# Two elementwise products of a rational activation moved from VectorE to GpSimd

## The chip, the cores and the metric

The kernel runs on one core of a Trainium2 chip. The metric is the device time of one execution in microseconds (us); the time before is the median of three executions.

## The reference

The program computes banded attention, a dense mixture of experts, and a feed-forward layer with a rational activation. The last one is where the change lies; `a` has four numbers, `b` two.

```python
def _moe2_ref(x, w_in, w_out, a, b):
    h = x @ w_in                      # 1152 x 512 by 512 x 2048
    h2 = h * h
    h3 = h2 * h
    P = a[0] + a[1] * h + a[2] * h2 + a[3] * h3
    Q = 1.0 + np.abs(b[0]) * np.abs(h) + np.abs(b[1]) * h2
    g = P / (Q + 1e-06)
    return (g @ w_out).astype(np.float32)
```

## The kernel before, in words

Tokens run in three chunks c = 0, 1, 2 of 384 columns. Hidden features run in units of 256, two units to a granule g; granules 0 to 7 (units 0 to 15) belong to the experts, granules 8 to 11 (units 16 to 23) to the rational layer. Float32 operands of the large products are split into a high and a low part, and three passes carry high by high, high by low and low by high. So an activation has two products: `hh`, the high part, and `hl`, the low part.

A unit of a chunk, written (u, c) here, goes like this. TensorE makes its hidden features in one PSUM tile (`h_bank`, L319, 48 matmuls for two units). The activation then makes `hh` and `hl`. Later TensorE multiplies these by the second weights, a token tile at a time (`o_half`, L356): for each of three token tiles, unit u's `hh` four times, its `hl` twice, then unit u+1's `hh` four times and its `hl` twice. DVE adds the result to the sum (`o_sum`, L384 or L386).

The activation is the class `Rational` (L418 to L467). Its steps, named after its methods, are:

- `first`: three ScalarE instructions (L430 to L432) that read the PSUM tile: the square, |b0 h|, and the start of the numerator.
- `denominator`: one DVE instruction (L435) that joins square and absolute value, then Ln and Exp on ScalarE (L439, L440).
- `numerator`: two DVE instructions (L444, L445), each with one operand in PSUM. The second frees the PSUM tile.
- `third`: two DVE instructions (L450, L453), a Newton step on the reciprocal, both operands in SBUF.
- `fourth`: one DVE instruction (L458), both operands in SBUF, and ScalarE's copy that makes `hh` (L462).
- `fifth`: one DVE instruction (L465) that makes `hl` from the result and `hh`.

Each engine takes its instructions in the order in which the program is written (`manual_schedule`, L469). `h_step` and `o_step` (L614, L638) set that order. An even unit's `denominator`, `numerator` follow at once behind its `first`, but behind `third` and `fourth` of the odd unit of the pair before; the odd unit's `fifth` comes between the even unit's `denominator` and `numerator`. The even unit's `third`, `fourth`, `fifth` and the odd unit's `denominator`, `numerator` are put between the token tiles of the next `o_step`. In the steady part a period is two units and three token tiles, 16.54 us. The entry into the rational layer (L661 to L675, and the `extra` turns of x at L690 to L692) and the last chunk (L715 to L755) are written out by hand.

Of the kernel before, what the change touches and what calls it, by code (L numbers as in the profile page):

```python
"""Banded attention, a dense mixture of experts and a rational-activation MLP, in one launch.

Tokens run in three chunks of 384 columns; the middle one has the first 192 tokens of both batches.
For a chunk, a plain head has six blocks of 64 queries against 96 keys, and a dilated head eight of
48 queries against 80 keys, two for each residue of the position, within which its band is plain.
Float32 operands of the large products are split into two float32r parts each
(x = hi + lo exactly), and three passes carry hi*hi + hi*lo + lo*hi.
"""
# [2 lines left out]

# [17 lines left out]
NT, DM = 1152, 512  # L29
E, FE = 4, 1024  # L30
F2 = 2048
# blocks of a chunk, their queries and their keys: plain and dilated heads
BLOCKS = ((6, 64, 96), (8, 48, 80))
TC = 384
NCH = 3
# [1 line left out]
WINDOW, DIL = 32, 4  # L37
NG1, NG = 2 * E, 2 * E + F2 // 512
QSCALE = 1.0 / D ** 0.5
NORMAL64 = float(np.uint32(897 << 20).view(np.float32))  # high word of the double 2**-126  # L40


@with_exitstack
def body(ctx, tc, qkv, mask, dp, w1, w2, w1d, w2d, coef, out):
# [10 lines left out]
    third = []  # L55

    def h_tile(count=[0]):
        """Two banks; a third pair joins once the attention has left it."""
        count[0] += 1
        pool = third[0] if third and count[0] % 3 == 0 else psh  # L60
        return pool.tile([128, 2, 512], F32, tag="h", name="ps_h")
# [11 lines left out]

    nc.scalar.preload_act_table_set("natural_log_exp_and_others")

# [1 line left out]
    w1s, w2s, scratch = {}, {}, {}  # L77

    def load_w(src, store, nm):
# [28 lines left out]
    split_w1, split_w2 = split_w(w1s, "w1"), split_w(w2s, "w2")  # L108

    def weight(store, u, n):  # L110
        """hi and lo of a unit's weights as n row groups."""
        return (store[u][:, i].rearrange("p (k f) -> p k f", k=n) for i in range(2))

# [1 line left out]
    def convert(pool):  # L115
        pieces = []
        for u in range(2 * NG1, 2 * NG, 2):
            for nm, src in (("w1", w1d), ("w2", w2d)):
                for v_ in (u, u + 1):
                    scratch[nm, v_] = dram.tile([128, 2, 1024], F32, tag=f"{nm}_{v_}", name=f"{nm}_{v_}")  # L120
                    for i in range(2):
                        pieces.append((src[v_ - 2 * NG1], scratch[nm, v_], slice(i * 512, (i + 1) * 512)))

        def load(n):
            src, _, s = pieces[n]
            x = pool.tile([128, 512, 2], U32, tag="x64", name="x64")
            nc.sync.dma_start(x.rearrange("p a b -> p (a b)"), src.bitcast(U32)[:, 2 * s.start:2 * s.stop])
            return x

        nxt = load(0)  # L130
        for n, (_, dst, s) in enumerate(pieces):
            x, nxt = nxt, load(n + 1) if n + 1 < len(pieces) else None
            low, high = x[:, :, 0], x[:, :, 1]
            t = pool.tile([128, 512], U32, tag="t", name="t")
            e = pool.tile([128, 512], U32, tag="e", name="e")
            f = pool.tile([128, 512], F32, tag="f", name="f")
            mag = pool.tile([128, 512], F32, tag="mag", name="mag")
            w = pool.tile([128, 2, 512], F32R, tag="w", name="w")
            nc.scalar.activation(mag, high.bitcast(F32), AF.Abs)
            # sign, exponent and the upper 20 bits of the fraction  # L140
            nc.vector.tensor_scalar(
                out=t, in0=high, scalar1=3, scalar2=0x3FFFFFF8,
                op0=ALU.logical_shift_left, op1=ALU.bitwise_and,
            )
            yield
            nc.vector.scalar_tensor_tensor(
                out=t, in0=high, scalar=0xC0000000, in1=t, op0=ALU.bitwise_and, op1=ALU.bitwise_or
            )
            yield
            # the lower 32 bits of the fraction, scaled by the signed power of two  # L150
            nc.vector.tensor_scalar(
                out=e, in0=t, scalar1=0xFF800000, scalar2=None, op0=ALU.bitwise_and
            )
            nc.vector.scalar_tensor_tensor(
                out=f, in0=low, scalar=2.0 ** -52, in1=e.bitcast(F32), op0=ALU.mult, op1=ALU.mult
            )
            yield
            nc.vector.tensor_tensor(out=f, in0=f, in1=t.bitcast(F32), op=ALU.add)
            yield
            # below float32's normal range: zero  # L160
            nc.vector.scalar_tensor_tensor(  # L161
                out=f, in0=mag, scalar=NORMAL64, in1=f, op0=ALU.is_ge, op1=ALU.mult
            )
            nc.scalar.copy(w[:, 0], f)  # L164
            yield
            nc.vector.tensor_tensor(out=w[:, 1], in0=f, in1=w[:, 0].bitcast(F32), op=ALU.subtract)  # L166
            nc.sync.dma_start(dst[:, :, s], w.bitcast(F32))
            yield

# [1 line left out]
    xt = {}  # L171

    def new_x(c):
# [2 lines left out]
        xt[c] = (xh, xl)  # L176

    class Attn:
        """A chunk's pair of heads; the steps up to the transposes run a head (half) at a time.

        A block's scores have its queries on partitions, those of odd blocks from 64 up.
        """

        def __init__(self, c, p):
            self.c, self.p = c, p
# [120 lines left out]
                    out=dst(xl), in0=src, in1=dst(xh.bitcast(F32)), op=ALU.subtract  # L306
                )

# [1 line left out]
    hs = {}  # L310
    acc = {}

# [32 lines left out]
        return [(0, 128, 128 * t)]  # L345

    def o_half(g, t, v, ps):
        """A token tile's products with one unit's 256 features."""
        c, j = divmod(t, 3)
        tk = slice(j * 128, (j + 1) * 128)  # L350
        hh, hl = hs[2 * g + v, c]
# [9 lines left out]
        return pso.tile([128, 512], F32, tag="o", name="ps_o")  # L361

    def o_tile(g, t, ps=None):
        """A token tile's products with a granule; the sum too, unless the caller's bank holds them."""
        held, ps = ps is not None, ps if ps is not None else o_bank()
        for v in range(2):
            o_half(g, t, v, ps)
        if not held:
            o_sum(g, t, ps)
# [21 lines left out]
    x2_ps = {}  # L391

    def x2_turn(c, half):
        """Two of the four feature groups of a chunk, turned features-first."""
        if half == 0:
            new_x(c)
        ps = x2_ps[c, half] = h_tile()
# [18 lines left out]
        x2_split(c, half)  # L416

    class Rational:  # L418
        """g = P(h) / (Q(h) + 1e-6): 1/Q from exp(-ln Q) and a Newton step, P negated with it."""
        pool = None  # L420

        def __init__(self, u, c, ps):
            self.u, self.c, self.ps = u, c, ps

        def first(self):
            ps = self.ps[:, :, :TC]
            self.sq = self.pool.tile([128, 2, TC], F32, tag="sq", name="sq")
            self.ab = self.pool.tile([128, 2, TC], F32, tag="ab", name="ab")
            self.u1 = self.pool.tile([128, 2, TC], F32, tag="u1", name="u1")
            nc.scalar.activation(self.sq, ps, AF.Square)  # L430
            nc.scalar.activation(self.ab, ps, AF.Abs, scale=absb[:, 0:1])  # L431
            nc.scalar.activation(self.u1, ps, AF.Identity, scale=na[:, 3:4], bias=na[:, 2:3])  # L432

        def denominator(self):
            nc.vector.scalar_tensor_tensor(  # L435
                out=self.sq, in0=self.sq, scalar=absb[:, 1:2], in1=self.ab,
                op0=ALU.mult, op1=ALU.add,
            )
            nc.scalar.activation(self.ab, self.sq, AF.Ln, bias=cbias)  # L439
            nc.scalar.activation(self.ab, self.ab, AF.Exp, scale=-1.0)  # L440

# [20 lines left out]
            nc.scalar.copy(self.hh, self.u1)  # L462

        def fifth(self):
            nc.vector.tensor_tensor(  # L465
                out=self.hl, in0=self.u1, in1=self.hh.bitcast(F32), op=ALU.subtract
            )  # L467

    with tc.manual_schedule():  # L469
# [9 lines left out]
        ps_h = {}  # L479

        def h_k(k, u):
            """The k-th quarter of granule 0 on chunk 0."""
            if k == 0:
                ps_h[u] = h_tile()
            for i in range(2):
# [57 lines left out]
            21: [part(split_w2, 3, 1)],  # L543
        }

        # TensorE's clock falls when little of it is used, as in the first steps of the attention
        warm = const.tile([128, 512], BF16, name="warm")
        nc.vector.memset(warm, 0.0)
        ps_w = h_tile()
# [98 lines left out]
        for g in range(NG):  # L648
# [63 lines left out]
                x2_half(0, 0)  # L712
                x2_half(0, 1)
            o_step(g, 1)
        # the last chunk's hidden features come before the products that wait for nothing  # L715
        u, g = 2 * NG - 2, NG - 1
        r = []
        for v in range(2):
            r.append(Rational(u + v, 2, h_tile()))
            for i in range(2):  # L720
                h_bank(u + v, 2, i, r[v].ps)
            for f in between.pop(0):
# [36 lines left out]


def _slots():
    """Where each chunk's pair of heads starts in the array of windows, and the array's size."""
    at, slot = 0, {}
    for c in range(NCH):
        for p in range(NPAIR):
# [7 lines left out]


def _window(c, kind, b):
    """Batch, queries and keys (S for none) of a block."""
    _, qb, kb = BLOCKS[kind]
    if kind == 0:
        t = 64 * (b % 3) if c == 1 else 192 + 64 * b
# [7 lines left out]


def _mask():
    """Added to the raw scores: nothing, or -1e9 before the scale."""  # L790
    from ml_dtypes import bfloat16

    m = np.zeros((2, 64, 4, 320), np.float32)
# [59 lines left out]
```

## Time and profile before

| | us |
|---|---|
| time, median of 3 executions (667.65 to 669.11) | 668.04 |
| profiled execution, span from first to last instruction | 667.8 |
| TensorE matmul busy in the span | 654.5 (98%) |
| DVE busy | 496.5 (74%) |
| ScalarE (ACT) busy | 269.1 (40%) |
| GpSimd (POOL) busy | 17.6 (3%) |
| granted TensorE clock, mean | 0.994 |

The profile gives the profiled execution's span alone; its time is this span and what lies around it, about 0.2 us by the median. Matmuls are pipelined, so TensorE's busy share is not its share of peak; what is read here is where it waits. PE is TensorE's matmul, PEld its weight load. A row of the timeline reads: start, duration, engine, line, operation, result and operands, and in brackets how long the engine was idle before and what ended that.

### The profile page before, as it was taken

Reading aid. Unit: us, or ns where it says so; the run is one execution under the profiler, and the core shown is the slowest. Engines: PE = TensorE matmul, PEld = TensorE weight load, DVE = VectorE, ACT = ScalarE, POOL = GpSimd, SP = SyncE. Lnnn points to the kernel's source line nnn. Section 1 sums busy time; section 2 is a strip of 40 time slices with the busy share of each in tenths; the row PEclk is TensorE's granted clock in tenths of the full one; section 3 lists DMA queues with packets and bytes.
Section 4 is the critical chain, followed back from the end, with each engine's and each line's share of the span. In section 5 each row is a group of like instructions: output and inputs, shape, how many; then the busy total and the mean of one; then the engine's idle time right before and its main releaser. Section 6 shows DMA issues by size and latency. Waiting matters only on the chain.

```text
span 667.8 us, 9561 instructions
## 1 busy us (share of the span) xinstructions
PE 654.5 (98%) x3845; PEld 586.5 (88%) x3845; DVE 496.5 (74%) x760; ACT 269.1 (40%) x510; POOL 17.6 (3%) x30
## 2 busy tenths in 40 slices
PE   6899999999999999999999999999999999999997
PEld 4788889899999999999999999999999999999985
DVE  3597653796886786786786786634899999999986
ACT  3465441242232332332322322214656555555551
POOL 1111110000000000000000000000000000000000
PEclk9799999999999999999999999999999999999999
DMA  8746201262652552562562573540330330300012
GB/s 242 243 148 210 89 1 64 79 211 90 190 168 85 189 175 88 179 189 84 169 189 94 159 239 112 185 158 0 127 113 14 127 127 0 128 1 0 1 49 94
DMA packets 25149, 80.27 MB, mean 120 GB/s; under 512 B 2672, under 2 KB 2928, under 8 KB 23056
## 3 DMA queue, kind: packets, MB, share of 16 engines
q1 hardware_dynamic: 24528, 79.31, 37.0%
q8 instruction: 30, 0.49, 0.3%
q10 hardware_dynamic: 576, 0.35, 0.3%
q14 instruction: 15, 0.12, 0.1%
HBM read 60.51 MB, written 19.14 MB: 119 GB/s over the span
## 4 chain that ended last, share of the span: by engine, by line
PE 93%; DMA 3%; DVE 3%; ACT 1%; SPq 0%; issue 0%; POOLq 0%
PE ps_h L319 45%; PE ps_o L356 41%; DMA qk<-in_qkv_dram 3%; PE ps_s L217 2%; PE ps_v L279 2%; PE ps_t L263 1%; PE ps_h L401 1%; PE ps_h L356 0%; ACT xh L304 0%; DVE xl L305 0%; PE ps_s L213 0%; DVE u L445 0%; DVE acc L386 0%; DVE u L458 0%; DVE sq L453 0%; DVE sq L450 0%
## 5 line engine op out<-in xcount | busy, mean ns | idle before, releaser
L319 PE MATMUL ps_h<-xh,w 128*128 128x384 f32 x1152 | 303.4, 338 | 0.1
L356 PE MATMUL ps_o<-w,hh 128*128 128x512 f32 x832 | 224.2, 391 | 0.5 <-DVE acc L378 0.5
L319 PEld LDWEIGHTS ps_h<-xh,w 128*128 128x128 f32 x1152 | 209.9, 189 | 2.6 <-ACT xh L304 0.3
L319 PE MATMUL ps_h<-xl,w 128*128 128x384 f32 x576 | 193.8, 336 | 0.7 <-DVE xl L305 0.6
L356 PEld LDWEIGHTS ps_o<-w,hh 128*128 128x128 f32 x832 | 155.2, 188 | 31.6 <-DVE acc L378 0.7
L356 PE MATMUL ps_o<-w,hl 128*128 128x512 f32 x416 | 128.5, 390 | 0.0
L319 PEld LDWEIGHTS ps_h<-xl,w 128*128 128x128 f32 x576 | 108.7, 189 | 2.6 <-DVE xl L305 1.5
L333 DVE SCALAR_TENSOR_TENSOR hl<-ps_h,hh 128x768 fp32r<-128x768 f32 x48 | 45.9, 955 | 66.3 <-ACT hh L332 66.3
L356 PEld LDWEIGHTS ps_o<-w,hl 128*128 128x128 f32 x416 | 78.1, 188 | 16.7
L332 ACT ACTIVATE hh<-ps_h 128x768 fp32r<-128x768 f32 x48 | 39.1, 815 | 117.3 <-PE ps_h L319 117.2
L164 ACT CAST w<-f 128x512 fp32r<-128x512 f32 x32 | 19.9, 621 | 123.6 <-DVE f L161 123.6
L380 DVE SCALAR_TENSOR_TENSOR acc<-ps_o,p_sb,acc 128x512 f32<-128x512 f32 x63 | 47.1, 748 | 11.5 <-PE ps_o L356 11.5
L102 DVE TENSOR_TENSOR w<-raw,w 128x512 fp32r<-128x512 f32 x64 | 41.6, 682 | 1.2 <-ACT w L101 1.2
L166 DVE TENSOR_TENSOR w<-f,w 128x512 fp32r<-128x512 f32 x32 | 22.1, 692 | 22.8 <-ACT w L164 22.8
L101 ACT CAST w<-raw 128x512 fp32r<-128x512 f32 x64 | 37.1, 620 | 1.6 <-DMA raw<-in_w_dram 1.6
L240 ACT ACTIVATE pr<-ps_s,nmx 128x80 f32<-128x80 f32 (+1 forms) x84 | 26.9, 335 | 26.9 <-DVE nmx L231 26.1
L439 ACT ACTIVATE ab<-sq,cbias 128x768 f32<-128x768 f32 x24 | 22.7, 944 | 37.2 <-DVE sq L435 37.0
L430 ACT ACTIVATE sq<-ps_h 128x768 f32<-128x768 f32 x24 | 19.3, 803 | 32.4 <-PE ps_h L319 32.4
L435 DVE SCALAR_TENSOR_TENSOR sq<-sq,absb,ab 128x768 f32<-128x768 f32 x24 | 24.3, 1012 | 3.8 <-ACT ab L431 3.8
L465 DVE TENSOR_TENSOR hl<-u,hh 128x768 fp32r<-128x768 f32 x24 | 22.9, 953 | 5.4 <-ACT hh L462 5.4
L217 PEld LDWEIGHTS ps_s<-qk 64*48 64x48 f32 (+1 forms) x336 | 15.4, 141 | 12.2 <-DMA qk<-in_qkv_dram 7.5
L445 DVE SCALAR_TENSOR_TENSOR u<-u,na,ps_h 128x768 f32<-128x768 f32 x24 | 24.3, 1014 | 0.8
(63 smaller groups left out, 566.1 us busy)
## 6 DMA issues: line engine op xcount, KB each, us to landing
raw<-in_w_dram SPq DMA_DIRECT2D x32, 512.0 KB, 6.1
w<-w SPq DMA_DIRECT2D x32, 512.0 KB, 3.6
w<-w SPq DMA_DIRECT2D x16, 1024.0 KB, 5.4
x<-in_w1d_dram SPq DMA_DIRECT2D x16, 512.0 KB, 5.4
x<-in_w2d_dram SPq DMA_DIRECT2D x16, 512.0 KB, 5.2
qk<-in_qkv_dram SPq DMA_DIRECT2D x6, 512.0 KB, 6.0
qk<-in_qkv_dram SPq DMA_DIRECT2D x5, 480.0 KB, 7.8
out_dram<-acc SPq DMA_DIRECT2D x8, 256.0 KB, 2.2
```

The costliest lines, as they stand in the source:

```text
L101: nc.scalar.copy(w[:, 0, s], raw[:, s])
L102: nc.vector.tensor_tensor(out=w[:, 1, s], in0=raw[:, s], in1=w[:, 0, s].bitcast(F32), op=ALU.subtract)
L217: nc.tensor.matmul(ps[64 * o:64 * o + self.qb, i * self.kb:(i + 1) * self.kb], lhsT=self.qk[r, b, :self.qb], rhs=self.qk[r, b, self.qb:], ...
L240: nc.scalar.activation(pr[:, i], sc[:, i], AF.Exp, scale=QSCALE, bias=nmx[:, i:i + 1], accum_out=total[:, i:i + 1],)
L319: nc.tensor.matmul(ps[:, i, :TC], lhsT=a[:, k, f], rhs=b[:, k], start=k + n == 0, stop=k + n == 5,)
L332: nc.scalar.activation(hh, ps[:, :, :TC], AF.Relu)
L333: nc.vector.scalar_tensor_tensor(out=hl, in0=ps[:, :, :TC], scalar=0.0, in1=hh.bitcast(F32), op0=ALU.max, op1=ALU.subtract,)
L356: nc.tensor.matmul(ps, lhsT=a[:, i, tk], rhs=b[:, i], start=v + n == 0, stop=v + n == 6)
L380: nc.vector.scalar_tensor_tensor(out=acc[t], in0=ps, scalar=pe, in1=acc[t], op0=ALU.mult, op1=ALU.add)
L435: nc.vector.scalar_tensor_tensor(out=self.sq, in0=self.sq, scalar=absb[:, 1:2], in1=self.ab, op0=ALU.mult, op1=ALU.add,)
L445: nc.vector.scalar_tensor_tensor(out=self.u1, in0=self.u1, scalar=na[:, 1:2], in1=ps, op0=ALU.add, op1=ALU.mult)
L465: nc.vector.tensor_tensor(out=self.hl, in0=self.u1, in1=self.hh.bitcast(F32), op=ALU.subtract)
```

## The change

In `first`, ScalarE now makes |h| from PSUM into `ab`, and from that `|b1||h| + |b0|` into `sq` (scale and bias in one instruction). `denominator` multiplies the two with a plain product, which with the constant added under the logarithm is the same denominator. That product and the difference in `fifth` go to GpSimd, except for the last chunk's two units, which are given `nc.vector`. The file's line numbers behind L425 are three lower. (Comments and docstrings, which the diff also takes out, are left out.)

```diff
-        def __init__(self, u, c, ps):
-            self.u, self.c, self.ps = u, c, ps
+        def __init__(self, u, c, ps, spare=nc.gpsimd):
+            self.u, self.c, self.ps, self.spare = u, c, ps, spare
...
-            nc.scalar.activation(self.sq, ps, AF.Square)
-            nc.scalar.activation(self.ab, ps, AF.Abs, scale=absb[:, 0:1])
+            nc.scalar.activation(self.ab, ps, AF.Abs)
+            nc.scalar.activation(self.sq, self.ab, AF.Identity, scale=absb[:, 1:2], bias=absb[:, 0:1])
             nc.scalar.activation(self.u1, ps, AF.Identity, scale=na[:, 3:4], bias=na[:, 2:3])
 
         def denominator(self):
-            nc.vector.scalar_tensor_tensor(
-                out=self.sq, in0=self.sq, scalar=absb[:, 1:2], in1=self.ab,
-                op0=ALU.mult, op1=ALU.add,
-            )
+            self.spare.tensor_tensor(out=self.sq, in0=self.sq, in1=self.ab, op=ALU.mult)
             nc.scalar.activation(self.ab, self.sq, AF.Ln, bias=cbias)
...
         def fifth(self):
-            nc.vector.tensor_tensor(
+            self.spare.tensor_tensor(
                 out=self.hl, in0=self.u1, in1=self.hh.bitcast(F32), op=ALU.subtract
             )
...
-            r.append(Rational(u + v, 2, h_tile()))
+            r.append(Rational(u + v, 2, h_tile(), nc.vector))
```

DVE's order at the entry into the rational layer, before. The unit (17, 0) has the tiles `sq_4373`, `u1_4375`, `hl_4456`; (16, 1) has `sq_4446`, `u1_4448`.

```order
L380 SCALAR_TENSOR_TENSOR acc8_1619<-ps_o_4400,p_sb_85,acc8_1619 128x512
L435 SCALAR_TENSOR_TENSOR sq_4373<-sq_4373,absb_89,ab_4374 128x768
L444 TENSOR_TENSOR u1_4375<-ps_h_4348,u1_4375 128x768
L445 SCALAR_TENSOR_TENSOR u1_4375<-u1_4375,na_88,ps_h_4348 128x768
L450 SCALAR_TENSOR_TENSOR sq_4373<-sq_4373,cbias_90,ab_4374 128x768
L453 SCALAR_TENSOR_TENSOR sq_4373<-sq_4373,ab_4374 128x768
L458 SCALAR_TENSOR_TENSOR u1_4375<-u1_4375,na_88,sq_4373 128x768
L435 SCALAR_TENSOR_TENSOR sq_4446<-sq_4446,absb_89,ab_4447 128x768
L465 TENSOR_TENSOR hl_4456<-u1_4375,hh_4455 128x768
L444 TENSOR_TENSOR u1_4448<-ps_h_4421,u1_4448 128x768
```

The same stretch of DVE's order in the change.

```order
L380 SCALAR_TENSOR_TENSOR acc8_1619<-ps_o_4400,p_sb_85,acc8_1619 128x512
L441 TENSOR_TENSOR u1_4375<-ps_h_4348,u1_4375 128x768
L442 SCALAR_TENSOR_TENSOR u1_4375<-u1_4375,na_88,ps_h_4348 128x768
L447 SCALAR_TENSOR_TENSOR sq_4373<-sq_4373,cbias_90,ab_4374 128x768
L450 SCALAR_TENSOR_TENSOR sq_4373<-sq_4373,ab_4374 128x768
L455 SCALAR_TENSOR_TENSOR u1_4375<-u1_4375,na_88,sq_4373 128x768
L441 TENSOR_TENSOR u1_4448<-ps_h_4421,u1_4448 128x768
```

Three instructions have left this stretch; what stays on DVE keeps its order. GpSimd's order in the change begins, behind the attention's products, with these rows (`sq_4337` and `hl_4397` belong to (16, 0); `sq_4500` and `hl_4554` to (17, 1) and (16, 1)).

```order
L435 TENSOR_TENSOR sq_4337<-sq_4337,ab_4338 128x768
L462 TENSOR_TENSOR hl_4397<-u1_4339,hh_4396 128x768
L435 TENSOR_TENSOR sq_4373<-sq_4373,ab_4374 128x768
L435 TENSOR_TENSOR sq_4446<-sq_4446,ab_4447 128x768
L462 TENSOR_TENSOR hl_4456<-u1_4375,hh_4455 128x768
L435 TENSOR_TENSOR sq_4500<-sq_4500,ab_4501 128x768
L462 TENSOR_TENSOR hl_4554<-u1_4448,hh_4553 128x768
```

Behind these, product and difference alternate to the end, 22 of each. An odd unit's difference stands behind the product of the even unit that comes after it, as it stood on DVE.

## Rows read from the trace of the kernel before

**Rows 1.** The page, part 1: busy time of each engine over the span.

```profile
PE 654.5 (98%) x3845; PEld 586.5 (88%) x3845; DVE 496.5 (74%) x760; ACT 269.1 (40%) x510; POOL 17.6 (3%) x30
```

**Rows 2.** Busy time in the rational layer: PE, PEld, DVE, ACT, POOL, clock, DMA.

```profile
457.00:653.00 196.00, 196.00 (x1005) 179.27 (x1004) 176.13 (x198) 118.86 (x146) 0.00 (x0) 1.00 0.16 58
```

**Rows 3.** Chain of work that ended last, in order of time, 470 to 540 us.

```profile
480.02 2.77 PE ps_o L356 x12
...
497.26 8.20 PE ps_o L356 x36
505.47 8.34 PE ps_h L319 x48
```

**Rows 4.** Groups of instructions by line and shape: count, busy us, mean ns, idle before.

```profile
L435 DVE SCALAR_TENSOR_TENSOR sq<-sq,absb,ab 128x768 f32<-128x768 f32 x24 | 24.3, 1012 | 3.8 <-ACT ab L431 3.8
L432 ACT ACTIVATE u<-ps_h,na 128x768 f32<-128x768 f32 x24 | 23.9, 995 | 0.0
L465 DVE TENSOR_TENSOR hl<-u,hh 128x768 fp32r<-128x768 f32 x24 | 22.9, 953 | 5.4 <-ACT hh L462 5.4
L439 ACT ACTIVATE ab<-sq,cbias 128x768 f32<-128x768 f32 x24 | 22.7, 944 | 37.2 <-DVE sq L435 37.0
L440 ACT ACTIVATE ab<-ab 128x768 f32<-128x768 f32 x24 | 20.3, 848 | 0.8
```

**Rows 5.** The same view, engine POOL: the attention's products.

```profile
L251 POOL TENSOR_TENSOR pr<-pr,rs 128x320 f32<-128x320 f32 x12 | 8.9, 741 | 42.8 <-DVE rs L250 38.0 <-ACT w L101 4.8
L251 POOL TENSOR_TENSOR pr<-pr,rs 128x288 f32<-128x288 f32 x12 | 8.0, 666 | 41.5 <-DVE rs L250 39.5 <-PE ps_s L217 2.0
```

**Rows 6.** Timeline of DVE and POOL in three places of the attention.

```profile
27.72 0.17 DVE L231 TENSOR_SCALAR nmx<-mx 128x4 f32<-128x4 f32 x1
...
36.29 0.43 DVE L230 TENSOR_REDUCE mx<-ps_s 128x3 f32<-128x288 f32 x1
36.55 0.72 POOL L251 TENSOR_TENSOR pr<-pr,rs 128x320 f32<-128x320 f32 x1 [2.78 <-DVE rs L250]
36.76 0.54 DVE L231 TENSOR_SCALAR nmx<-mx 128x3 f32<-128x3 f32 x1
...
95.61 0.66 DVE L102 TENSOR_TENSOR w<-raw,w 128x512 fp32r<-128x512 f32 x1
95.86 0.98 POOL L251 TENSOR_TENSOR pr<-pr,rs 128x320 f32<-128x320 f32 x1 [3.71 <-DVE rs L250]
```

**Rows 7.** Timeline of PE: odd unit's two parts, entry and a steady period.

```profile
481.25 1.08 PE L356 MATMUL ps_o<-w,hh 128*128 128x512 f32 x4
482.16 0.62 PE L356 MATMUL ps_o<-w,hl 128*128 128x512 f32 x2
...
532.50 0.62 PE L356 MATMUL ps_o<-w,hl 128*128 128x512 f32 x2
```

**Rows 8.** Timeline of ACT and DVE: units (16, 0) and (17, 0), then a steady period.

```profile
461.38 0.81 ACT L430 ACTIVATE sq<-ps_h 128x768 f32<-128x768 f32 x1 [3.34 <-PE ps_h L319]
...
472.42 1.01 DVE L435 SCALAR_TENSOR_TENSOR sq<-sq,absb,ab 128x768 f32<-128x768 f32 x1
...
477.42 1.02 DVE L458 SCALAR_TENSOR_TENSOR u<-u,na,sq 128x768 f32<-128x768 f32 x1
...
478.47 0.84 ACT L462 CAST hh<-u 128x768 fp32r<-128x768 f32 x1 [0.76 <-DVE u L458]
...
479.34 0.96 DVE L465 TENSOR_TENSOR hl<-u,hh 128x768 fp32r<-128x768 f32 x1
...
526.23 0.81 ACT L430 ACTIVATE sq<-ps_h 128x768 f32<-128x768 f32 x1 [3.51 <-PE ps_h L319]
...
529.47 0.96 DVE L465 TENSOR_TENSOR hl<-u,hh 128x768 fp32r<-128x768 f32 x1 [0.51 <-ACT hh L462]
```

**Rows 9.** Timeline of the tail: DVE's difference, and PE's last wait.

```profile
645.01 0.95 DVE L465 TENSOR_TENSOR hl<-u,hh 128x768 fp32r<-128x768 f32 x1
...
658.94 1.20 PE L356 MATMUL ps_h<-w,hh 128*128 128x512 f32 x4 [0.38 <-ACT hh L462]
```

## The prediction

> **What bounds the kernel now.** I read the page's busy shares first: PE 98%, DVE 74%, POOL 3% [rows 1]. A share over the whole span decides nothing, so next come the windows of the rational layer: from 457 to 653 us PE is busy 196.0 of 196.0 us, DVE 176.1, ACT 118.9, POOL 0, and the clock is full [rows 2]. The chain of waits says the same: over this stretch it is PE alone, three token tiles in 8.20 us and two units in 8.34 us, in turn [rows 3], with no other engine in between. So DVE, though 90% busy, holds nobody up there, and taking work off it is worth nothing in itself. The only place where PE waits in this layer is the tail: 0.38 us for the last unit's `hh` [rows 9], and some 0.1 us more for its neighbours.
>
> **What the change moves.** 22 products of 1.01 us and 22 differences of 0.95 us leave DVE [rows 4], 43 us of its 176. They cost the path nothing now, so removing them gains nothing on the path, except in the tail. There one moved difference (0.95 us, a step of 0.87 to the next start) lies in DVE's run of work up to the last `hh` [rows 9]. It can give back what PE waits for, 0.38 us plus about 0.1. Two more products stay on DVE but become plain ones, 0.06 us shorter each. The gain is thus bounded by 0.5 us, and the term I take is -0.1, because GpSimd would run the difference just as DVE wants its next two-input instruction (below).
>
> **What GpSimd takes for one.** No row shows a 768-element product on POOL. The two shapes there are 320 elements in 741 ns and 288 in 666 ns [rows 5]. In proportion, 666 / 288 x 768 gives 1.78 us. A line through the usual 0.72 us of the 320 shape [rows 6] and 0.67 of the 288 has a slope of about 1.65 ns an element and gives 0.72 + 448 x 0.00165 = 1.46 us. These are the ends; I take the middle, 1.62, so each is 0.6 us longer than on DVE. The Trainium skill, GPSIMD Engine Reference, section on elementwise work side by side, gives 4497 ns for 2048 elements, which in proportion is an estimate of 1.69 us; no run here shows it yet, and the sum below would be +3.9 by it.
>
> ScalarE's `first` now has a dependent second instruction. Its form lies between L440 (848 ns) and L432 (995 ns); I take 0.95 and a start right behind the end of the first. `sq` is ready 1.8 us after the PSUM tile, and ACT, busy 118.9 of 196, has room.
>
> **The port.** POOL and DVE do not run freely side by side. DVE's tiny L231 takes 0.17 us alone, but 0.54 when POOL's product is under way, and ends at 37.30, as that product does at 37.27; L230, which reads PSUM, is not stretched (0.43) [rows 6]. The other way round, POOL's product of 0.72 us takes 0.98 when it starts 0.25 us into DVE's L102, which has two SBUF operands [rows 6]. I therefore assume that POOL's instruction and a DVE one with two SBUF operands take turns (`third`, `fourth`), while `numerator` and the sums, with one operand in PSUM, run beside it. The Trainium skill, SBUF — State Buffer, section "Who interferes with whom", states an exclusive lock for the whole instruction; these rows agree (0.26 us and 0.37 us lost). Without turns the sum would be about -0.2 (the entry's `hl` 0.3 late, the tail's 0.5 back) instead of +3.1.
>
> **The entry, walked.** In the steady part results have time to be late. At the entry they have little: (17, 0) has `hh` done at 479.31 and `hl` at 480.30 [rows 8], and PE takes them at 481.25 and 482.16 [rows 7]. Margins are 1.9 us. Now the new times, with 0.15 us for a hand-over to POOL.
> - (16, 0): |h| 461.38 to 462.19, `sq` to 463.2, POOL's product 463.3 to 464.9, Ln and Exp to 466.8, `third` to 468.8, sum to 469.5, `fourth` to 470.5, `hh` to 471.4, POOL's difference to 473.1.
> - (17, 0): its product stands behind that difference on POOL: 473.1 to 474.8 (before: it began at 472.42 and took 1.01 [rows 8]). Ln, Exp to 476.7; `third` 476.8 to 478.75.
> - Meanwhile ACT's `first` of (16, 1) is pushed behind that Exp, and its `sq` is ready at 478.5, so POOL asks at 478.7, while DVE is still in `third`. When that ends, POOL, which has been waiting, goes first: 478.7 to 480.3. DVE's `fourth` starts at 480.3 rather than at 477.42 [rows 8], `hh` is done at 482.2: **1.0 us late** for PE. POOL's difference runs 482.35 to 484.0; PE, already shifted, wants it at 483.1: **0.9 us late** more.
>
> That makes +1.9. The lateness goes on: ACT's and DVE's split of the third chunk's x lies next in both queues, so DVE reaches `third` of (17, 1) only at 495.3 to 497.3. POOL asks for (16, 2)'s product at 496.8 and is again served before `fourth`. `fourth` 498.85, `hh` 500.75 against 500.4 wanted, difference 500.9 to 502.5 against 501.7 (these wants are 497.26 [rows 3] plus 1.2 and 2.1, as 481.25 and 482.16 [rows 7] stand to 480.02 [rows 3], plus what is lost by then): 0.4 and 0.9, **+1.3** together. After that DVE, 43 us lighter over the layer, has caught up, and `fourth` ends before POOL asks.
>
> **Steady part.** With `first` at 526.23 [rows 8], product 528.2 to 529.8, difference to 531.5; it was done at 530.43. PE takes it at 532.50 [rows 7]: 1 us of margin, no cost. It runs out when POOL takes 2.1 us.
>
> Sum: 1.9 + 1.3 - 0.1 = +3.1, made against the span of 667.8, whose surround (0.2 us to the median of 668.04) I leave as it is: 668.04 + 3.1 = **671.1 us**.
>
> **The rivals.**
> - *Cover holds, the tail gains.* The two engines share the port without whole-instruction turns, or POOL is near 1.46 and DVE is served first. Then (17, 0) `hl` ends at 482.2 or before and PE hardly waits; the tail gives up to 0.5. Time 667.5 to 668.3. For: the only two-operand case in the trace cost POOL 0.26 us, less than L102's 0.66. Against: L231 was held to the very end of POOL's instruction.
> - *DVE first.* The port goes to DVE's next instruction. `fourth` runs at 478.75, `hh` is in time at 480.6, but the product ends at 481.3 and the difference at 483.0: 0.8 late, and 0.6 at the second place. Sum +1.4 less 0.1: 669.4. No row shows both asking at once. I hold POOL-first the likelier, since in [rows 6] the one that had begun was served to its end and POOL would have asked before `fourth` is due, but not by much.
> - *A loss in each period.* If POOL takes 2.1 us or more, or if `fourth` of the odd unit comes to stand behind the next product in the steady part too (it ends within about 0.3 us of that request in my walk), then `hl` is late in each of some 10 periods of 16.54 us, by 0.5 to 1.5 us: 5 to 15 us on top, 673 to 686.
>
> **How the numbers follow.** A measurement of this kernel tells a change from none at about 0.2%, 1.3 us. Forecast, both places with POOL first: 0.45, 670.3 to 672.5 from 1.46 to 1.78 us. DVE first: 0.24, 668.0 to 670.8, of which two thirds are slower by over 1.3 us. Cover holds: 0.22. Loss in each period: 0.09. Slower by over 0.2%: 0.45 + 0.16 + 0.09 = 0.70, less 0.03 for measurement. Faster needs over 1.3 us, and PE has 0.5 to give: 0.04, for what I overlooked. Same: 0.29. The range leaves out the loss in each period beyond 673.8 and little at the lower end: 667.5 to 673.8.
>
> **What would show it.** Right: PE waits at (17, 0) and (17, 1), first for ACT's `hh`, then for POOL's `hl`, some 3 us in all, and no wait in the steady part; POOL rows of about 1.6 us, longer where `third` or `fourth` runs; DVE busy some 133 us where it was 176. Wrong: PE busy without a gap from 457 to 653, or waits that recur every 16.54 us, or POOL's instruction outside 1.46 to 1.78 us.

## The result and the profile after

The change makes the kernel slower: 673.29 us (672.69 to 673.94, four executions) against 667.94 us, a ratio of 1.0071 with a 95% interval of 1.0052 to 1.0089. A second series, run with the experiments, gave 671.97 us against 667.64 us and again 1.0071 (1.0057 to 1.0085). These ratios are estimates over all executions, not quotients of the medians, which are 5.4 and 4.3 us apart. By the ratio the loss is 4.7 us, 3.5 to 5.9 by the first interval.

The forecast was 671.1 us in a range of 667.5 to 673.8. Both medians lie in the range; the first lies above the 670.3 to 672.5 that the forecast's own case (both places, GpSimd first) allowed.

The busy time of the rational layer, with the same columns as [rows 2], then its entry, then the time from there to 660 us:

```profile
457.00:653.00 196.00, 193.87 (x993) 176.63 (x992) 153.38 (x151) 123.64 (x143) 83.33 (x44) 1.00 0.16 57
457.00:500.00 43.00, 40.95 (x221) 37.67 (x220) 28.71 (x32) 26.38 (x31) 14.91 (x8) 1.00 0.20 72
500.00:660.00 160.00, 159.92 (x803) 144.18 (x802) 131.56 (x128) 101.03 (x116) 68.42 (x37) 1.00 0.15 52
```

TensorE, without a gap before, now lacks 2.1 us there, and 2.05 of that lie ahead of 500 us, at the entry. From 500 to 660 us it is as full as before. The waits of its weight loads (PEld) in the layer say on whom it waits (engine and tile waited for, total us, times, longest):

```profile
PEld ps_o L356 <- ACT hh L459: 1.8, 1, 1.8
PEld ps_o L356 <- POOL hl L462: 1.7, 2, 1.1
```

PE's timeline shows the place, the first token tile that uses granule 8 (unit 17's `hh` and `hl` are the third and fourth row). Before, its second row, which goes ahead of the two in [rows 7], was this:

```profile
480.78 0.63 PE L356 MATMUL ps_o<-w,hl 128*128 128x512 f32 x2
```

In the change the four are these:

```profile
480.24 1.08 PE L356 MATMUL ps_o<-w,hh 128*128 128x512 f32 x4
481.16 0.63 PE L356 MATMUL ps_o<-w,hl 128*128 128x512 f32 x2
483.13 1.21 PE L356 MATMUL ps_o<-w,hh 128*128 128x512 f32 x4 [1.34 <-ACT hh L459]
485.05 0.73 PE L356 MATMUL ps_o<-w,hl 128*128 128x512 f32 x2 [0.71 <-POOL hl L462]
```

Before, the `hh` pass followed the `hl` pass by 0.47 us, now by 1.97; from there to unit 17's `hl` it took 0.91, now 1.92. So 1.5 and 1.0 us are lost in this one tile, by the starts of its passes; the gaps alone, 1.34 and 0.71, say less, because the ends of matmuls are modelled. The margin of 1.9 us was used up before that: GpSimd runs the product of (17, 0) only behind the difference of (16, 0), and `third` of (17, 0) starts, counted from the start of the layer (below), 1.9 us later than before. The first two rows are GpSimd's, then come `third`'s first step in the change and, last, in the kernel before.

```profile
472.08 1.86 POOL L462 TENSOR_TENSOR hl<-u,hh 128x768 fp32r<-128x768 f32 x1 [6.51 <-ACT hh L459]
473.88 1.84 POOL L435 TENSOR_TENSOR sq<-sq,ab 128x768 f32<-128x768 f32 x1
```

```profile
477.68 1.02 DVE L447 SCALAR_TENSOR_TENSOR sq<-sq,cbias,ab 128x768 f32<-128x768 f32 x1 [3.60 <-ACT ab L437]
```

```profile
475.37 1.02 DVE L450 SCALAR_TENSOR_TENSOR sq<-sq,cbias,ab 128x768 f32<-128x768 f32 x1
```

What comes on top is on DVE, GpSimd and ScalarE, in that order:

```profile
478.73 0.96 DVE L450 SCALAR_TENSOR_TENSOR sq<-sq,ab 128x768 f32<-128x768 f32 x1
479.73 2.49 DVE L455 SCALAR_TENSOR_TENSOR u<-u,na,sq 128x768 f32<-128x768 f32 x1
```

```profile
479.42 1.99 POOL L435 TENSOR_TENSOR sq<-sq,ab 128x768 f32<-128x768 f32 x1 [3.69 <-ACT sq L431]
483.16 1.84 POOL L462 TENSOR_TENSOR hl<-u,hh 128x768 fp32r<-128x768 f32 x1 [1.75 <-ACT hh L459]
```

```profile
482.25 0.83 ACT L459 CAST hh<-u 128x768 fp32r<-128x768 f32 x1 [2.03 <-DVE u L455]
```

GpSimd asks for the product of (16, 1) while DVE is in `third` of (17, 0). It is held for 0.14 us (1.99 instead of 1.85), then DVE's `fourth` is held behind it: 2.49 us for an instruction that took 1.02 [rows 8]. `hh` comes 1.5 us late, and the difference, 1.84 us on GpSimd, another 1.0.

The second loss is in the tail, where the last chunk's own product stays on DVE:

```profile
646.86 0.69 DVE L386 TENSOR_TENSOR acc<-ps_o,acc 128x512 f32<-128x512 f32 x1 [0.76 <-PE ps_o L356]
647.47 2.29 DVE L435 TENSOR_TENSOR sq<-sq,ab 128x768 f32<-128x768 f32 x1
```

It is held by the last difference on GpSimd, which runs from 647.10 to 648.94:

```profile
647.10 1.84 POOL L462 TENSOR_TENSOR hl<-u,hh 128x768 fp32r<-128x768 f32 x1 [3.34 <-issue]
```

So 1.34 us go into DVE's run of work, where the moved difference had freed 0.87.

For size I count a stretch that leaves the attention's part out. It goes from the start of the second turn of x into the layer (L401; 455.68 us before, 456.06 after) to the start of the second sum of the last granule (643.48 and 646.86), and a second one from there to the end of the span. The first two rows are of the kernel before, the third of the change:

```profile
455.68 1.47 PE L401 MATMUL ps_h<-ident,acc 128*128 128x128 f32 x12
643.48 0.69 DVE L386 TENSOR_TENSOR acc<-ps_o,acc 128x512 f32<-128x512 f32 x1 [1.10 <-PE ps_o L356]
```

```profile
456.06 1.47 PE L401 MATMUL ps_h<-ident,acc 128*128 128x128 f32 x12
```

In the kernel before the two take 187.80 and 24.32 us, after 190.80 and 24.74. So the entry costs 3.0 us, 2.5 of them in the tile above, and the tail 0.4.

GpSimd's instructions, by line and shape (count, busy us, mean ns, idle before), answer to [rows 5]:

```profile
L435 POOL TENSOR_TENSOR sq<-sq,ab 128x768 f32<-128x768 f32 x22 | 42.2, 1917 | 408.9 <-ACT sq L431 408.9
L462 POOL TENSOR_TENSOR hl<-u,hh 128x768 fp32r<-128x768 f32 x22 | 41.6, 1891 | 53.9 <-issue 33.7 <-ACT hh L459 20.2
```

Most of them take 1.84 to 1.85 us, more than the 1.78 that I gave as the upper end.

### The profile page after: what moved, and what is told of

Read it like the earlier page. It is cut to its first block, busy times and chain, and to the rows that moved or that the text cites. A ratio compares the mean times of both kernels' runs of the same rounds, so it can differ in the third digit from the quotient of the medians.

```text
span 671.6 us, 9617 instructions
## 1 busy us (share of the span) xinstructions
PE 657.1 (98%) x3845; PEld 587.2 (87%) x3845; DVE 477.5 (71%) x716; ACT 276.4 (41%) x510; POOL 100.9 (15%) x74
## 4 chain that ended last, share of the span: by engine, by line
PE 82%; DVE 6%; issue 5%; DMA 3%; ACT 2%; POOL 2%; SPq 0%; POOLq 0%; DVEq 0%; ACTq 0%
PE ps_h L319 40%; PE ps_o L356 36%; DMA qk<-in_qkv_dram 2%; PE ps_s L217 2%; PE ps_v L279 2%; PE ps_t L263 1%; POOL sq L435 1%; DVE u L455 1%; POOL hl L462 1%; DVE sq L447 1%; DVE sq L450 1%; ACT hh L459 1%; PE ps_h L356 0%; DVE sq L435 0%; DMA w<-w 0%
## 5 line engine op out<-in xcount | busy, mean ns | idle before, releaser
L435 POOL TENSOR_TENSOR sq<-sq,ab 128x768 f32<-128x768 f32 x22 | 42.2, 1917 | 408.9 <-ACT sq L431 408.9
L462 POOL TENSOR_TENSOR hl<-u,hh 128x768 fp32r<-128x768 f32 x22 | 41.6, 1891 | 53.9 <-issue 33.7
L447 DVE SCALAR_TENSOR_TENSOR sq<-sq,cbias,ab 128x768 f32<-128x768 f32 x24 | 37.5, 1561 | 5.5 <-ACT ab L437 5.5
L441 DVE TENSOR_TENSOR u<-ps_h,u 128x768 f32<-128x768 f32 x24 | 22.8, 952 | 12.7 <-ACT u L432 12.7
L430 ACT ACTIVATE ab<-ps_h 128x768 f32<-128x768 f32 x24 | 19.3, 803 | 29.3 <-PE ps_h L319 29.3
```

Source lines behind the costliest of these rows:

```text
L435: self.spare.tensor_tensor(out=self.sq, in0=self.sq, in1=self.ab, op=ALU.mult)
L441: nc.vector.tensor_tensor(out=self.u1, in0=ps, in1=self.u1, op=ALU.mult)
L447: nc.vector.scalar_tensor_tensor(out=self.sq, in0=self.sq, scalar=cbias, in1=self.ab, op0=ALU.add, op1=ALU.mult)
L462: self.spare.tensor_tensor(out=self.hl, in0=self.u1, in1=self.hh.bitcast(F32), op=ALU.subtract)
```

## The experiments

Theory 1 is that of the prediction: GpSimd's instructions are long and take turns with DVE's two-operand ones, which makes two odd units late at the entry and holds DVE in the tail. Against it stand a loss from the new form of the denominator (rival A), a loss from GpSimd's use wherever it lies (rival B), and long instructions without turns (rival C). The runs' table gives the stretch as defined above. The first four experiments below ran with the series whose time before is 668.26, the others with that of 667.64; the change itself is compared with 667.94, as above.

| kernel | time, us | ratio to before (95%) | entry to last granule | from there to the end |
|---|---|---|---|---|
| before | 668.26, 667.64 in the two series | | 187.80 | 24.32 |
| the change | 673.29 | 1.0071 (1.0052 to 1.0089) | 190.80 | 24.74 |
| the change again | 671.97 | 1.0071 (1.0057 to 1.0085) | 191.70 | 24.66 |
| form only | 668.42 | 1.0005 (0.9994 to 1.0015) | 187.80 | 24.24 |
| entry on DVE | 669.05 | 1.0011 (1.0001 to 1.0021) | 187.80 | 24.74 |
| entry and last pair on DVE | 668.70 | 1.0015 (1.0002 to 1.0028) | 187.80 | 24.27 |
| product only on GpSimd | 676.32 | 1.0122 (1.0109 to 1.0136) | 195.80 | 24.19 |
| difference only on GpSimd | 668.50 | 1.0012 (0.9999 to 1.0026) | 188.08 | 24.40 |
| two products on DVE | 669.04 | 1.0031 (1.0014 to 1.0048) | 188.92 | 24.70 |
| halves | 670.87 | 1.0055 (1.0041 to 1.0069) | 190.50 | 24.65 |

**Form only.**

```diff
-        def __init__(self, u, c, ps, spare=nc.gpsimd):
+        def __init__(self, u, c, ps, spare=nc.vector):
```

> Only the new form of the denominator stays; product and difference are on DVE for all 24 units. Late hand-overs (theory 1: the change's loss is GpSimd's 1.85 us instructions being late at the first two odd units, and one of them holding DVE in the tail): TensorE waits nowhere between 457 and 653 us, and the time is within 0.5 us of the kernel before. Rival A (the new form itself costs, since |h| and the scaled copy now depend on one another on ScalarE): 1 us or more above the kernel before.

The ratio is 1.0005, with 1 inside its interval, and TensorE has no gap:

```profile
457.00:653.00 196.00, 196.00 (x1003) 179.06 (x1003) 175.88 (x200) 124.59 (x145) 0.00 (x0) 1.00 0.16 58
```

The dependent step on ScalarE costs that engine some 6 us of busy time (118.9 to 124.6) and the path nothing. Rival A falls.

**Entry on DVE.**

```diff
-            r = Rational(u, c, ps)
+            r = Rational(u, c, ps, nc.vector if u < 18 else nc.gpsimd)
```

> Granule 8's units (16 and 17, all chunks) keep product and difference on DVE; the other units have them on GpSimd as in the change. Theory 1: the two waits of TensorE at the entry are gone (some 2.8 us of its idle time), what is left is the tail: 0.3 to 0.8 us above the kernel before in the span. Rival B (GpSimd's use costs wherever it lies, by slowing DVE and ScalarE or outside the span): 3 to 5 us above the kernel before, in proportion to the 32 of 44 instructions that remain.

The entry is back at 187.80 us, the tail stays at 24.74. The time is 0.8 us above before. With 32 of 44 instructions still on GpSimd, the steady part is free of any loss:

```profile
457.00:653.00 196.00, 196.00 (x1004) 179.18 (x1004) 164.50 (x166) 126.03 (x146) 60.74 (x32) 1.00 0.16 58
```

Rival B, which wanted 3 to 5 us, falls.

**Entry and last pair on DVE.**

```diff
-            r = Rational(u, c, ps)
+            r = Rational(u, c, ps, nc.vector if u < 18 or (u >= 22 and c == 1) else nc.gpsimd)
```

> As the run before, and units 22 and 23 of the middle chunk on DVE too, so that no GpSimd instruction lies beside the tail. Theory 1: TensorE's waits are those of the kernel before; the span within 0.3 us of it, and 28 instructions are still on GpSimd. Rival B: 2 to 4 us above.

Now the tail is back too: 24.27 us. DVE's product there takes 0.95 us instead of the 2.29 of the change:

```profile
641.13 0.69 DVE L386 TENSOR_TENSOR acc<-ps_o,acc 128x512 f32<-128x512 f32 x1 [1.10 <-PE ps_o L356]
641.74 0.95 DVE L435 TENSOR_TENSOR sq<-sq,ab 128x768 f32<-128x768 f32 x1
```

In the stretch this kernel equals the one before. Its time is 0.4 us above by the medians, with an interval that just excludes 1, and its profiled execution has a span of 665.4 us, the one of before 667.8. So the excess does not lie in the stretch. Four of its twelve executions ran at a mean granted clock of 0.993 to 0.994 and took 669.8 to 670.3 us, against three of 29 below 0.995 for the kernel before; the medians of the others are 668.4 and 668.2. In the one profile with such a mean, that of the kernel before, the granted clock is 0.50 (1.2 GHz, the lower of its two levels) from 26 to 30 us, after PE had waited 1.7 us for an input of the attention, and full in the layer [rows 2]. In all the profiles together the layer begins anywhere from 450.8 to 456.1 us, so the part ahead of it alone moves by several us from one execution to the next.

**Product only on GpSimd.**

```diff
-            self.spare.tensor_tensor(
+            nc.vector.tensor_tensor(
                 out=self.hl, in0=self.u1, in1=self.hh.bitcast(F32), op=ALU.subtract
             )
```

> The product on GpSimd, the difference on DVE. Theory 1 with turns at the port: DVE now carries 21 us more, so the odd unit's last two-operand step comes to stand behind the next product in every period, and TensorE waits in each: 6 to 12 us above the kernel before. Without turns at the port (rival C: GpSimd's instructions are only long, and do not hold DVE): at most the entry's loss, 0 to 3 us above.

1.0122, 8.0 us in the stretch: with half as many instructions on GpSimd the loss is about twice that of the whole change. This is the prediction's loss in each period, made to happen. The chain of work that ended last has left PE for DVE, and repeats itself (start, us, engine, tile, line):

```profile
528.50 0.94 DVE sq L447
529.46 0.97 DVE sq L450
530.46 2.50 DVE u L455
532.98 0.84 ACT hh L459
533.84 0.96 DVE hl L462
```

Of the 22 products on GpSimd, 19 hold one of DVE's two-operand steps for about 1.5 us, ten times `fourth` (L455). Rival C gave this run 3 us at most, and falls.

**The change again.** The same file once more.

> The change itself once more, for the size of the loss and where it lies. Counted from the start of token tiles 7 and 8 at the entry to the end of the span, the kernel before takes 202.3 us and the change took 205.7, so theory 1 expects +3.4 us there, 671.5 to 672.2 us in all if nothing else is lost. Rival B expects some 673.3 again, with 1.5 us or more that lie outside this stretch.

The stretch lost 4.2 us in this execution (3.9 at the entry, 0.3 in the tail) where 3.4 was expected, the times 4.3. So in this execution nearly all of the loss lies in the stretch, and the 0.8 us by which the two profiles of the same kernel differ have a place. At (17, 1) the first execution had

```profile
498.06 1.02 DVE L455 SCALAR_TENSOR_TENSOR u<-u,na,sq 128x768 f32<-128x768 f32 x1
...
498.11 2.68 POOL L435 TENSOR_TENSOR sq<-sq,ab 128x768 f32<-128x768 f32 x1 [1.89 <-ACT sq L431]
```

and this one

```profile
495.73 2.67 DVE L455 SCALAR_TENSOR_TENSOR u<-u,na,sq 128x768 f32<-128x768 f32 x1
...
495.75 1.84 POOL L435 TENSOR_TENSOR sq<-sq,ab 128x768 f32<-128x768 f32 x1 [1.86 <-ACT sq L431]
```

Two requests within 0.02 to 0.05 us: in the first DVE goes first and GpSimd is held for 0.83 us, in the second the other way round. PE then loses 0.25 us there (1.16 from `hh` to `hl` instead of 0.91) or 1.2 (0.2 for `hh`, 1.0 for `hl`).

**Difference only on GpSimd.**

```diff
-            self.spare.tensor_tensor(out=self.sq, in0=self.sq, in1=self.ab, op=ALU.mult)
+            nc.vector.tensor_tensor(out=self.sq, in0=self.sq, in1=self.ab, op=ALU.mult)
```

> The difference on GpSimd, the product (plain, two operands) on DVE. Theory 1: it is the product, asked for while the odd unit's last two-operand step is due, that holds up the chain; without it the differences alone cost 0.3 to 1.2 us in the stretch from the entry to the end, the tail's 0.4 among them. Rival B: half of the change's loss, 1.7 us or more.

0.3 us at the entry, 0.1 in the tail. The product is what holds up the chain, as expected. The difference follows `fourth`, which keeps its 1.01 to 1.02 us in all 24 units; it meets the first step of `third` (L447, over 1.3 us in ten of 24) without a cost in the stretch. This run takes 21 us of work off DVE, whose busy time falls from 176.1 to 162.9 us, and gains nothing.

**Two products on DVE.**

```diff
-            self.spare.tensor_tensor(out=self.sq, in0=self.sq, in1=self.ab, op=ALU.mult)
+            eng = nc.vector if (self.u, self.c) in ((16, 1), (16, 2)) else self.spare
+            eng.tensor_tensor(out=self.sq, in0=self.sq, in1=self.ab, op=ALU.mult)
```

> The change, but the products of (16, 1) and (16, 2), the two that lay beside the odd unit's chain at the entry, on DVE; 42 of 44 instructions stay on GpSimd. Theory 1: the wait for hh at (17, 0) and the wait at (17, 1) go, the wait for hl at (17, 0) of about 1 us and the tail's 0.4 stay: +1.4 us in the stretch where the change has +3.4. Rival B: no more than a twentieth of the loss goes, +3.2.

The stretch lost 1.5 us (1.1 and 0.4) where 1.4 was expected. With 42 of 44 instructions left on GpSimd, more than half of the first execution's loss of 3.4 us and two thirds of the second's 4.2 are gone. The wait for `hh` is gone with them; PE's wait for `hl` at (17, 0) stays:

```profile
476.37 1.20 PE L356 MATMUL ps_o<-w,hh 128*128 128x512 f32 x4
478.29 0.73 PE L356 MATMUL ps_o<-w,hl 128*128 128x512 f32 x2 [0.73 <-POOL hl L463]
```

**Halves.**

```diff
-            self.spare.tensor_tensor(out=self.sq, in0=self.sq, in1=self.ab, op=ALU.mult)
+            for i in range(2):
+                self.spare.tensor_tensor(
+                    out=self.sq[:, i], in0=self.sq[:, i], in1=self.ab[:, i], op=ALU.mult
+                )
```

and the same for the difference.

> The change with each GpSimd instruction cut into two of 384 elements, so that a turn at the port is half as long: 0.95 us. Theory 1 with turns in the order of asking: DVE's fourth at (17, 0) waits for half a product only and hh comes 0.8 to 1.0 us sooner, hl as late as before: the stretch takes 0.7 to 1.5 us less than the change, unless the second instruction's start costs it. Without turns: as the change or longer.

At the entry DVE's `fourth` (L458 in this file) is held for half a product only, 1.65 us in all instead of 2.49, and goes between the halves, which take 2.82 together instead of 2.0:

```profile
479.12 1.65 DVE L458 SCALAR_TENSOR_TENSOR u<-u,na,sq 128x768 f32<-128x768 f32 x1
```

```profile
478.82 2.82 POOL L436 TENSOR_TENSOR sq<-sq,ab 128x384 f32<-128x384 f32 x2 [3.70 <-ACT sq L431]
```

PE waits 0.92 us for `hh` where it waited 1.34. In all the stretch lost 3.0 us, 0.4 to 1.2 less than in the two profiles of the change, and the time is 1.1 us below it. That lies around the lower end of what was expected for the stretch. For `hh` it is less than expected: it comes 0.4 us sooner, not 0.8 to 1.0. The hold did shrink by 0.84 us. But two halves, 1.00 us each at the least, take some 0.15 us longer than one whole, and with three such pairs ahead of it `fourth` starts 0.4 us later, counted from the start of the layer.

## Why the prediction was right, and where it was not

- **What bounds the kernel** held: difference only took one instruction in each unit off DVE (21 us less work), and TensorE came no earlier.
- **The entry** was the place, with the mechanism as walked: the margin used up by GpSimd's longer instructions, then GpSimd served as `third` ends, `fourth` held, `hh` late, then `hl`. The sizes of its parts were off. At (17, 0) I had 1.0 and 0.9, measured 1.5 and 1.0; at (17, 1) I had 0.4 and 0.9, measured 0 and 0.25 in one execution, 0.2 and 1.0 in the other. The entry's 3.2 thus became 3.0 and 3.9. That the sum came so near in the first execution is luck: the first place, taken too small, and the second, taken too large, made up for one another.
- **What GpSimd takes for one** was the term that was mis-sized: 1.62 us, in a range up to 1.78, measured 1.84 to 1.85. So one of the prediction's own signs of being wrong came true, and with it the walk was some 0.2 us too early at each of GpSimd's instructions. The likely reason, which no run tests by itself, is that the attention's product is not a plain one; its second operand repeats one element. Two whole-row products of 384 and 768 elements (1.00 us at the least in halves, 1.84 in the change) give 2.19 ns an element and 0.16 us fixed, by which 320 elements would take 0.86 us; the attention's take 0.72 [rows 6]. The Trainium skill, GPSIMD Engine Reference, in its section on elementwise work side by side, gives 4497 ns for 2048 elements; the estimate of 1.69 us from it was nearer, and still 0.15 short.
- **The port** was read rightly: the rows of one small DVE instruction and one disturbed product stood for the whole. Who goes first was said to be GpSimd, as the one that asks first. At (17, 0) it was; at (17, 1) both ask within hundredths and either may win, so the rival "DVE first" was not another case but a part of the same one.
- **The tail** had the wrong sign: -0.1, measured +0.4. That GpSimd would run the difference as DVE wants its product was seen, but I set the hold equal to what was freed. It is 1.34 against 0.87.
- **The steady part** held: PE's busy time from 500 to 660 us is as before. There the hold mostly falls on `third` instead of `fourth`: seven of the 24 L447 take over 2.6 us, at no cost. It holds by little, as product only shows.
- **The base** was a slip: I took 0.2 us around the span. Each execution that lists both has 1.74 to 1.87 us, so the span of 667.8 belongs to an execution above the median, and the 0.2 us set two different executions against each other. It moved nothing in the sum.
- DVE's busy time fell to 153 us, not to 133, because an instruction that is held counts as busy: L447 has a mean of 1.59 us in the layer where L450 of the kernel before had 1.01.

The two stalls' sum of 3.1 was 1 to 2 us short of the times. Of that, the stretch explains 0.3 in one profile and 1.1 in the other. The rest of the first series' median, 1 to 2 us, lies outside the stretch, where the part ahead of the layer moves by as much from one execution to the next; the second series does not show it, and its cause stays open.

No version beat the kernel before: where GpSimd's instructions are kept from the entry and the tail, the stretch is as long as it was, because TensorE is busy in all of it.

## What to carry to other kernels

Moving work to an idle engine pays only where the engine that is relieved ends a wait; look for that wait first, and count the extra time of a hand-over against the place where a result has least time to be late, which is the entry into a stage and not its steady part. Where the two engines take turns at a port, the moved instruction also lengthens the ones that stay, so half a move can cost more than the whole. A price from another shape may not be a bound when its operands are of another kind.

## What the runs showed of the hardware

- GpSimd's two-operand product of 128x768 float32 mostly takes 1.84 to 1.85 us, DVE's 0.95; the difference into a float32r tile takes the same on GpSimd.
- A GpSimd instruction and a DVE instruction with two SBUF operands take turns for nearly their whole length: DVE's 1.0 us became 2.3 to 2.7, GpSimd's 1.85 became up to 2.68. With one operand in PSUM DVE is not held: L442 keeps its 1.01 to 1.02 us beside them. The Trainium skill, SBUF — State Buffer, section "Who interferes with whom", says that a DVE instruction with two SBUF inputs contends with a GpSimd instruction that reads SBUF, and one with at most one does not; the trace agrees.
- When both ask within a few hundredths of a microsecond, the same kernel can go either way from one execution to the next, here with 0.8 us of difference.
